# A decode block on one core: the down projection's first 20 row chunks in loads of 12 and 8

## The chip, the core and the metric

The kernel runs on one core of one Trainium2 chip. A core has five engines with a queue of instructions each: TensorE (PE; its weight loads are listed apart as PEld), VectorE (DVE), ScalarE (ACT), GpSimd (POOL) and SyncE (SP), which here issues nearly all DMAs. The DMAs run on 16 DMA engines; a DMA of 128 partitions gives each of them eight rows, and loads that are queued one behind the other are worked off in order. The time is device time of one execution in microseconds, the median of several runs. Before the change it is 265.09 us (three runs, 264.94 to 265.29).

## What is computed

One decode step of a transformer block for 8 sequences: layer norm, attention of one new token over the last 1024 cached keys and values (32 query heads, 4 key/value heads of 128), the output projection with a residual, a second layer norm, and a gated feed-forward part, all in float32. The change is in the last product, `h @ w_down`.

```python
def _B_ref(x, w_gate, w_up, w_down):
    g = jnp.einsum("bsd,df->bsf", x, w_gate)     # 8 x 1024 times 1024 x 3584
    u = jnp.einsum("bsd,df->bsf", x, w_up)
    h = _gelu(g) * u
    return jnp.einsum("bsf,fd->bsd", h, w_down)  # 8 x 3584 times 3584 x 1024

h  = x + _A_ref(_layernorm(x), k_cache, v_cache, wq, wo)
h2 = h + _B_ref(_layernorm(h), w_gate, w_up, w_down)
```

## The kernel before

Every weight is used once, so the kernel is a row of loads into one large buffer, `space`, of 32 slots of 1024 float32 per partition (a slot holds one chunk of 128 rows of `w_down`), with matmuls behind them. The order of loads on SP's queue is written out by hand: `wq`, `kt`, `v`, `wo`, the first set of gate and up weights (4 column blocks of 512), the second set (3 column blocks), then `w_down`. A load waits for the matmuls that last read the slots it overwrites; SP works in order, so a load behind a waiting one waits too.

**The second set of the feed-forward part.** The gate weights of the second set lie in slots 0 to 11, the up weights in slots 12 to 23 (`place` counts them, and `base` is 24). The matmuls of L377 read them. `used[0, 1]` marks the last up matmul of the first set, `used[1, 0]` the last gate matmul of the second, `used[1, 1]` the last up matmul of the second.

**The down projection.** `w_down` has 28 chunks. `PARTS` (L27) says how they are loaded: 8, 8, 4, 4, 2, 1, and the last chunk in two column parts (`ends`, L448). Before the change chunk q lies in slot (24 + q) mod 32: chunks 0 to 7 in slots 24 to 31 (they wait for `used[0, 1]`), 8 to 19 in slots 0 to 11 (`used[1, 0]`), 20 and up from slot 12 on (`used[1, 1]`, L428). The load that ends with chunk 19 (`SIDE`, L430) leaves out the last 320 columns of that chunk; they come in eight small loads on four partitions each into `w_side` (L436), which SP issues just ahead of that load. A line of `move` (L92) issues every other load.

**The matmuls.** `h` is transposed into `at` (L189, L398, L401). PE can work on four groups of 32 output columns of its array at once; a result then lies four times in `ya`, 32 partitions each. First, L453 adds the residual `h_sb` into groups 0 and 1. Then L463 takes two chunks at a time: four products (two chunks, two halves of 512 columns). In a "slow" pair (`SLOW`, L36) the two chunks use the same two groups one after the other, in other pairs all four groups work at once. Each float32 product is two matmul rows in the profile. Behind chunk 19 the products of `w_side` (L473) fill in the missing columns in groups 1 and 3. DVE copies `ya` to `d1` (L478), PE adds its four parts into `acc` (L483, with `add2`) and goes on with chunks 20 to 26 in four quarters of 256 columns; ACT copies `acc` to `most` (L494); the two parts of the last chunk go to `tb` and `ta` (L505), DVE adds them to `most` (L508), and two DMAs write the output.

Of the kernel before, what the change touches and what calls it, by code (L numbers as in the profile page):

```python
# [15 lines left out]
NQ = 4  # L16
CP = 32 // B
QW = D // NQ
N = 512
# [4 lines left out]
SETS = (NQ, DF // N - NQ)  # L24


PARTS = (8, 8, 4, 4, 2, 1)  # L27
SIDE = 19
SIDE_COLS = 320
SIDE_ROWS = (0, 16, 64, 80)  # L30
ENDS = (160, 96)
FOLD = 20
AHEAD = 3


SLOW = (*range(0, 8), 16, 17)  # L36


class Flow:
# [42 lines left out]
    def run(self, engine, make, *waits, mark=True):  # L82
        ins = self.start(engine, make, waits)
        if not mark:
            return None
        self.done[engine] += 1
        ins.then_inc(self.own[engine], 1)
        return self.own[engine], self.done[engine]
# [7 lines left out]
def decode_block(nc, x, wq, kt, v, wo, gu, dn, side, ends, outs):  # L96
# [9 lines left out]
    run, move = fl.run, fl.move  # L106
# [31 lines left out]
    ta, tb, ya = bank("ta", N), bank("tb", N), bank("ya", N)  # L138
# [21 lines left out]
    w_side = sb("w_side", 64, len(SIDE_ROWS), SIDE_COLS)  # L160
# [68 lines left out]
    for hf in range(2):  # L229
        w, w_in, wb = wq_t[hf]  # L230
        q_ps = (acc, tb)[hf]
        for c in range(NC):
            for j in range(NQ):
                tok = run("tensor", lambda e, c=c, j=j: e.matmul(  # L234
                    q_ps[32 * j:32 * j + 32, :], xt[c], w[:, c, j * N:(j + 1) * N],
                    start=(c == 0), stop=(c == NC - 1)),
                    w_in, x_ok, mark=(c == NC - 1 and j == NQ - 1))
        free[wb] = tok
        q_sb = sb(f"q{hf}", P, N)
        tok = run("vector", lambda e: e.tensor_scalar(q_sb, q_ps, scale, None, op0=ALU.mult), tok)  # L240
        acc_free = tok
        qt, tok = transposes(ta, q_sb, N // P, tok, ta_free)
# [10 lines left out]
    for hf in range(2):  # L253
        s_ps = big[hf]
        k_t, k_in, wb = load(kt[hf], f"kt{hf}", "s b k", s=2, b=B)
        for b in range(HB):
            for k0 in range(0, W, N):
                for r in range(NQ):
                    s, half = divmod(r, 2)
                    c0 = 32 * b + 160 * half  # L260
                    end = b == HB - 1 and k0 + N == W and r == NQ - 1
                    tok = run("tensor", lambda e: e.matmul(  # L262
                        s_ps[32 * r:32 * r + 32, k0:k0 + N], qz[hf][:, s, c0:c0 + 32],
                        k_t[:, s, half * HB + b, k0:k0 + N],
                        start=(b == 0), stop=(b == HB - 1)), k_in, q_ok[hf], mark=end)
# [31 lines left out]
    for hf in range(2):  # L297
# [8 lines left out]
        for c in range(KC):  # L306
            for r in range(NQ):
                s, half = divmod(r, 2)
                tok = run("tensor", lambda e: e.matmul(  # L309
                    o3[32 * r:32 * r + 32], pt[:, c, 32 * r:32 * r + 32],  # L310
                    v_t[:, s, c, half * HB:(half + 1) * HB, :],
                    start=(c == 0), stop=(c == KC - 1)),
                    v_in, ta_free, ya_free, mark=(c == KC - 1 and r == NQ - 1))
# [15 lines left out]
    for hf in range(2):  # L329
# [4 lines left out]
        for h in range(0, 2 * REP, 2):  # L334
            for r in range(NQ):
                e2, ch = divmod(r, 2)
# [24 lines left out]
    q0 = 0  # L361
# [51 lines left out]
    SLOTS = 2 * BUF // D  # L413
    base = place // D

    def slot(q):
        return (base + q) % SLOTS

    def rows_of(q):
        return ring[:, slot(q)]  # L420
# [3 lines left out]
    for i, n in enumerate(PARTS):  # L424


        a, b = slot(q0), slot(q0) + n
        clear = used[0, 1] if a >= base else used[1, 0] if b * D <= place // 2 else used[1, 1]  # L428
        assert b <= SLOTS and (a >= base or b <= base)
        if q0 <= SIDE < q0 + n:  # L430
            assert SIDE == q0 + n - 1

            side_in = fl.sem("w_side")
            for h, src in enumerate(side):
                p0 = h % 4 + 32 * (h // 4)
                fl.start("sync", lambda e: e.dma_start(w_side[p0:p0 + 13:4], src), [zero[-1]]).then_inc(  # L436
                    side_in, 16)
            side_in = side_in, 16 * len(side)
            here = move(f"wd{i}", space[:, a * D:b * D - SIDE_COLS], dn[i], clear)
        else:  # L440
            here = move(f"wd{i}", ring[:, a:b], dn[i], clear)
        arrived.update((q, here) for q in range(q0, q0 + n))
        q0 += n
# [14 lines left out]
    for q in range(0, FOLD, 2):  # L458
        for i in range(NQ):
            e2, ch = divmod(i, 2)  # L460
            r = ch if q in SLOW else i
            n = N - SIDE_COLS if (q + e2, ch) == (SIDE, 1) else N
            run("tensor", lambda e: e.matmul(  # L463
                ya[32 * r:32 * r + 32, 0:n], at[:, q + e2, :],
                rows_of(q + e2)[:, ch * N:ch * N + n],
                start=(r not in opened), stop=(q == FOLD - 2 and ch == 0)),
                arrived[q + e2], at_ok[(q + e2) * P >= SETS[0] * N],
                mark=False)
            opened.add(r)
            if n < N:  # L470
                for s in range(len(SIDE_ROWS)):
                    r = 1 + 2 * (s % 2)
                    tok = run("tensor", lambda e: e.matmul(  # L473
                        ya[32 * r:32 * r + 32, n:N], at_side[:, s, :], w_side[0:48, s, :],
                        start=False, stop=(s >= len(SIDE_ROWS) - 2)), side_in, side_ok,
                        mark=(s == len(SIDE_ROWS) - 1))
    d1 = sb("d1", P, N)
    d1_ok = run("vector", lambda e: e.tensor_copy(d1, ya), tok)  # L478

# [131 lines left out]
```

## Time and profile before

| | before |
|---|---|
| median of three runs | 265.09 us (264.94 to 265.29) |
| the profiled execution, its time | 265.01 us |
| its span, first to last instruction | 263.7 us |
| PE busy | 139.5 us (53%) |
| DVE, ACT, POOL busy | 24.0, 10.8, 5.5 us |
| HBM read | 111.18 MB, 422 GB/s over the span |
| mean granted PE clock | 0.812 of full speed |

The profile is one execution on the chip, in microseconds from its first instruction. A row of the timeline gives the start, the length, the engine and line, what ran, out<-in with shapes, how many, and in brackets the engine's idle time ahead of it with what ended that. "DMA w<-dn" is the landing of a load of `w_down`. SPq rows are the issue of a DMA by SP, not its transfer. The chain of waits goes back from the last instruction, at each step to what released it. A stretch of the table of stretches gives, after its length, the busy time of PE, PEld, DVE, ACT and POOL, then the granted PE clock (1.00 is full speed, 0.50 half), the DMA share and GB/s. DMA bytes are put down to the stretch in which a packet starts, so a short stretch can show a share over 1.

### The profile page before, as it was taken

Reading aid. Unit: us, or ns where it says so; the run is one execution under the profiler, and the core shown is the slowest. Engines: PE = TensorE matmul, PEld = TensorE weight load, DVE = VectorE, ACT = ScalarE, POOL = GpSimd, SP = SyncE. Lnnn points to the kernel's source line nnn. Section 1 sums busy time; section 2 is a strip of 40 time slices with the busy share of each in tenths; the row PEclk is TensorE's granted clock in tenths of the full one; section 3 lists DMA queues with packets and bytes.
Section 4 is the critical chain, followed back from the end, with each engine's and each line's share of the span. In section 5 each row is a group of like instructions: output and inputs, shape, how many; then the busy total and the mean of one; then the engine's idle time right before and its main releaser. Section 6 shows DMA issues by size and latency. Waiting matters only on the chain.

```text
span 263.7 us, 2091 instructions
## 1 busy us (share of the span) xinstructions
PE 139.5 (53%) x966; PEld 40.8 (15%) x966; DVE 24.0 (9%) x59; ACT 10.8 (4%) x16; POOL 5.5 (2%) x15
## 2 busy tenths in 40 slices
PE   0015806804905916806706807818509667489876
PEld 0011201201201301301202202112102111123122
DVE  0320100100010020200200100160000200010011
ACT  1110000000010020110000000020000000000000
POOL 8000000000000000000000000000000000000000
PEclk9999975985965895975975956986965959799999
DMA  8997999999799989989998999899899989999995
GB/s 318 482 457 338 477 477 390 408 467 477 328 467 477 450 358 457 470 378 437 457 477 348 450 467 457 378 437 477 380 410 447 477 358 472 413 423 442 403 413 203
DMA packets 3256, 111.44 MB, mean 423 GB/s; under 512 B 520, under 2 KB 776, under 8 KB 1072
## 3 DMA queue, kind: packets, MB, share of 16 engines
q1 hardware_dynamic: 3088, 111.23, 98.1%
q8 instruction: 7, 0.11, 0.2%
q10 hardware_dynamic: 160, 0.08, 0.1%
q14 instruction: 1, 0.01, 0.0%
HBM read 111.18 MB, written 0.13 MB: 422 GB/s over the span
## 4 chain that ended last, share of the span: by engine, by line
DMA 78%; PE 20%; SPq 1%; issue 0%; DVE 0%
DMA w<-gu 20%; DMA w<-wq 16%; DMA w<-kt 12%; DMA w<-wo 11%; DMA w<-v 11%; DMA w<-ends 9%; PE big L377 6%; PE big L262 4%; PE tb L234 4%; PE tb L309 3%; PE ya L337 3%; SPq L92 1%; PE tb L505 0%; PE ta L505 0%; DVE o_fin L508 0%
## 5 line engine op out<-in xcount | busy, mean ns | idle before, releaser
L377 PE MATMUL big<-w,ln_t 128*32 128x512 f32 x224 | 36.8, 742 | 21.0 <-DMA w<-gu 21.0
L262 PE MATMUL big<-w,qz 128*32 128x512 f32 x128 | 19.1, 762 | 20.0 <-DMA w<-kt 20.0
L337 PE MATMUL ya<-w,ot 128*32 128x512 f32 x128 | 18.2, 732 | 19.4 <-DMA w<-wo 19.4
L377 PEld LDWEIGHTS big<-w,ln_t 128*32 128x32 f32 x224 | 9.2, 133 | 47.1 <-issue 26.3
L463 PE MATMUL ya<-w,at 128*32 128x512 f32 (+1 forms) x80 | 13.4, 588 | 2.1 <-DMA w<-dn 2.1
L309 PE MATMUL tb<-w,pt 128*32 128x512 f32 x64 | 9.1, 733 | 9.9 <-DMA w<-v 9.9
L234 PE MATMUL tb<-w,ln_t 128*32 128x512 f32 x64 | 9.3, 749 | 9.1 <-DMA w<-wq 9.1
L309 PE MATMUL acc<-w,pt 128*32 128x512 f32 x64 | 8.7, 703 | 8.5 <-DMA w<-v 8.5
L234 PE MATMUL acc<-w,ln_t 128*32 128x512 f32 x64 | 8.7, 705 | 7.5 <-DMA w<-wq 7.5
L189 PE MATMUL ta<-ident,ln_xn 64*128 64x64 f32 x16 | 2.0, 294 | 19.3 <-DVE ln_xn L215 19.3
L262 PEld LDWEIGHTS big<-w,qz 128*32 128x32 f32 x128 | 4.9, 137 | 33.4 <-issue 23.4
L337 PEld LDWEIGHTS ya<-w,ot 128*32 128x32 f32 x128 | 5.1, 132 | 31.1 <-issue 31.1
L390 DVE TENSOR_TENSOR hm<-ge,big 128x512 f32<-128x512 f32 (+1 forms) x2 | 1.4, 685 | 56.8 <-PE big L377 56.8
L271 DVE TENSOR_REDUCE nmax<-big 128x1 f32<-128x1024 f32 x2 | 2.4, 1224 | 35.7 <-PE big L262 35.7
L273 ACT ACTIVATE p<-big,nmax 128x1024 f32<-128x1024 f32 x2 | 2.2, 1115 | 78.2 <-DVE nmax L271 78.2
L463 PEld LDWEIGHTS ya<-w,at 128*32 128x32 f32 x80 | 3.6, 109 | 11.8 <-issue 9.8
L309 PEld LDWEIGHTS tb<-w,pt 128*32 128x32 f32 x64 | 2.5, 130 | 15.9 <-issue 15.9
L189 PEld LDWEIGHTS ta<-ident,ln_xn 64*128 64x128 f32 x16 | 1.6, 192 | 20.1 <-DVE ln_xn L215 20.1
L234 PEld LDWEIGHTS tb<-w,ln_t 128*32 128x32 f32 x64 | 2.3, 135 | 15.5 <-DMA w<-wq 9.3
L309 PEld LDWEIGHTS acc<-w,pt 128*32 128x32 f32 x64 | 2.4, 126 | 14.1 <-issue 14.1
L234 PEld LDWEIGHTS acc<-w,ln_t 128*32 128x32 f32 x64 | 2.4, 126 | 13.1 <-issue 13.1
L483 PE MATMUL acc<-w,at 128*32 128x256 f32 x56 | 3.6, 382 | 0.3 <-DMA w<-dn 0.3
(78 smaller groups left out, 54.0 us busy)
## 6 DMA issues: line engine op xcount, KB each, us to landing
w<-gu SPq DMA_DIRECT2D x2, 6144.0 KB, 23.7
w<-dn SPq DMA_DIRECT2D x2, 4096.0 KB, 26.9
w<-dn SPq DMA_DIRECT2D x1, 2048.0 KB, 20.0
w<-dn SPq DMA_DIRECT2D x1, 1888.0 KB, 23.7
w<-dn SPq DMA_DIRECT2D x1, 1024.0 KB, 22.1
w<-dn SPq DMA_DIRECT2D x1, 512.0 KB, 22.9
w<-ends SPq DMA_DIRECT2D x1, 320.0 KB, 23.2
w<-ends SPq DMA_DIRECT2D x1, 192.0 KB, 23.2
```

Source lines behind the costliest of these rows:

```text
L92: self.start(engine, lambda e: e.dma_start(out, src), waits).then_inc(s, 16)
L189: tok = run("tensor", lambda e, i=i: e.transpose(t[:, i, :], src[:, i * P:(i + 1) * P], ident[:rows, :rows]), id_ok, ready, clear, mark=(i ...
L234: tok = run("tensor", lambda e, c=c, j=j: e.matmul(q_ps[32 * j:32 * j + 32, :], xt[c], w[:, c, j * N:(j + 1) * N], start=(c == 0), stop=(c ...
L262: tok = run("tensor", lambda e: e.matmul(s_ps[32 * r:32 * r + 32, k0:k0 + N], qz[hf][:, s, c0:c0 + 32], k_t[:, s, half * HB + b, k0:k0 + N ...
L271: tok = run("vector", lambda e: e.tensor_reduce(out=nmax, in_=s_ps, axis=AX.X, op=ALU.max, negate=True), tok)
L273: p_ok = run("scalar", lambda e: e.activation(p_sb, s_ps, AF.Exp, bias=nmax, accum_out=tot), tok)
L309: tok = run("tensor", lambda e: e.matmul(o3[32 * r:32 * r + 32], pt[:, c, 32 * r:32 * r + 32], v_t[:, s, c, half * HB:(half + 1) * HB, :], ...
L337: tok = run("tensor", lambda e: e.matmul(ya[32 * r:32 * r + 32, :], ot[:, 2 * hf * REP + h + e2].rearrange("p r b -> p (r b)"), w[:, h + e ...
L377: tok = run("tensor", lambda e: e.matmul(pair[32 * j:32 * j + 32, s, :], ht[c], w[:, c, j * N:(j + 1) * N], start=(c == 0), stop=(c == NC ...
L390: tok = run("vector", lambda e: e.tensor_mul(hm[:rows], ge[:rows], pair[:rows, 1, :]), tok, g_ok)
L463: run("tensor", lambda e: e.matmul(ya[32 * r:32 * r + 32, 0:n], at[:, q + e2, :], rows_of(q + e2)[:, ch * N:ch * N + n], start=(r not in o ...
L483: tok = run("tensor", lambda e: e.matmul(acc[32 * j:32 * j + 32, 0:QW], lhs(j), rhs(j), start=start, stop=stop), *waits, mark=(stop and j ...
```

## The change

The first 20 chunks come in two loads, of 12 and 8 chunks, and the slots are dealt anew: chunks 0 to 11 lie in slots 0 to 11 (they wait for the gate matmuls of the second set, `used[1, 0]`), chunks 12 to 19 in slots 24 to 31 (`used[0, 1]`). The load that leaves out the 320 columns is now the one of 8 chunks, and the small side loads are issued ahead of it. Three pairs (chunks 0 to 5) are slow instead of five (0 to 7, 16 and 17). The side products run after chunk 11 instead of after chunk 19, and both halves of the last pair end their accumulation.

```diff
-PARTS = (8, 8, 4, 4, 2, 1)
+PARTS = (12, 8, 4, 2, 1)
...
-SLOW = (*range(0, 8), 16, 17)
+SLOW = tuple(range(0, 6))
+SIDE_AT = 10
...
+    first = PARTS[0]
+    places = [*range(first), *range(base, SLOTS), *range(first, base)]
+
     def slot(q):
-        return (base + q) % SLOTS
+        return places[q]
...
         a, b = slot(q0), slot(q0) + n
         clear = used[0, 1] if a >= base else used[1, 0] if b * D <= place // 2 else used[1, 1]
...
-            run("tensor", lambda e: e.matmul(
+            tok = run("tensor", lambda e: e.matmul(
                 ya[32 * r:32 * r + 32, 0:n], at[:, q + e2, :],
                 rows_of(q + e2)[:, ch * N:ch * N + n],
-                start=(r not in opened), stop=(q == FOLD - 2 and ch == 0)),
+                start=(r not in opened), stop=(q == FOLD - 2)),
                 arrived[q + e2], at_ok[(q + e2) * P >= SETS[0] * N],
-                mark=False)
+                mark=(q == FOLD - 2 and i == NQ - 1))
             opened.add(r)
-            if n < N:
-                for s in range(len(SIDE_ROWS)):
-                    r = 1 + 2 * (s % 2)
-                    tok = run("tensor", lambda e: e.matmul(
-                        ya[32 * r:32 * r + 32, n:N], at_side[:, s, :], w_side[0:48, s, :],
-                        start=False, stop=(s >= len(SIDE_ROWS) - 2)), side_in, side_ok,
-                        mark=(s == len(SIDE_ROWS) - 1))
+        if q == SIDE_AT:
+            assert opened == set(range(NQ))
+            for s in range(len(SIDE_ROWS)):
+                r = 1 + 2 * (s % 2)
+                run("tensor", lambda e: e.matmul(
+                    ya[32 * r:32 * r + 32, N - SIDE_COLS:N], at_side[:, s, :], w_side[0:48, s, :],
+                    start=False, stop=False), side_in, side_ok, mark=False)
```

More of the change, by code (lines that the diff above doesn't have):

```diff
@@ L428, in decode_block @@
         clear = used[0, 1] if a >= base else used[1, 0] if b * D <= place // 2 else used[1, 1]
+        assert [slot(q) for q in range(q0, q0 + n)] == list(range(a, b))
         assert b <= SLOTS and (a >= base or b <= base)
```

## The prediction

> **What bounds the kernel now.** I read the page first, then the chain of waits in order of time, then the timeline of the last 60 us, then the table of stretches.
>
> ```profile
> span 263.7 us, 2091 instructions
> ...
> q1 hardware_dynamic: 3088, 111.23, 98.1%
> ...
> DMA 78%; PE 20%; SPq 1%; issue 0%; DVE 0%
> ...
> 204.72 22.76 DMA w<-gu
> ...
> 237.67 23.19 DMA w<-ends
> ```
>
> SP's queue keeps the 16 DMA engines busy for 98.1% of the span, and the chain that ends last ends in a transfer: the last weights are issued at 237.67 and land 23.19 us later, because everything queued before them has to pass first. The page's 20% for PE in the chain is how long PE holds a buffer before the next load may be issued; it is no gap in the stream as long as another load is queued. So the kernel is one stream of 111 MB, and the change is worth what it does to the stream, unless it lets the stream run dry or makes PE late behind it.
>
> How close PE is behind the stream, the timeline tells (start, length, what ran, and in brackets the idle time before it):
>
> ```profile
> 212.94 9.25 PE L377 MATMUL big<-w,ln_t 128*32 128x512 f32 x48 [3.30 <-DMA w<-gu]
> ...
> 227.53 8.76 PE L377 MATMUL big<-w,ln_t 128*32 128x512 f32 x48 [5.34 <-DMA w<-gu]
> ...
> 237.86 1.05 PE L453 MATMUL ya<-h_sb,spread 128*32 128x512 f32 x4
> ...
> 238.74 7.04 PE L463 MATMUL ya<-w,at 128*32 128x512 f32 x32
> ...
> 246.95 3.64 PE L463 MATMUL ya<-w,at 128*32 128x512 f32 x32 [1.17 <-DMA w<-dn]
> ...
> 251.57 2.77 PE L463 MATMUL ya<-w,at 128*32 128x512 f32 x16 [0.98 <-DMA w<-dn]
> ...
> 254.27 1.27 PE L473 MATMUL ya<-w_side,at_side 48*32 48x320 f32 x8
> ...
> 255.58 0.69 DVE L478 COPY d<-ya 128x512 f32<-128x512 f32 x1 [17.06 <-PE ya L473]
> ...
> 256.33 0.64 PE L483 MATMUL acc<-d,add 128*32 128x256 f32 x8 [0.79 <-DVE d L478]
> ...
> 256.78 1.91 PE L483 MATMUL acc<-w,at 128*32 128x256 f32 x32
> ...
> 258.86 1.07 PE L483 MATMUL acc<-w,at 128*32 128x256 f32 x16 [0.17 <-DMA w<-dn]
> ...
> 260.11 0.64 PE L483 MATMUL acc<-w,at 128*32 128x256 f32 x8 [0.17 <-DMA w<-dn]
> ...
> 260.82 0.37 ACT L494 COPY most<-acc 128x256 f32<-128x256 f32 x1 [22.00 <-PE acc L483]
> 260.90 0.48 PE L505 MATMUL tb<-w,at 128*32 128x160 f32 x8 [0.15 <-DMA w<-ends]
> 261.38 0.37 PE L505 MATMUL ta<-w,at 128*32 128x96 f32 x8
> 261.45 0.32 DVE L508 TENSOR_TENSOR o_fin<-most,tb 128x160 f32<-128x160 f32 x1 [0.74 <-PE tb L505]
> ...
> 261.82 0.25 DVE L508 TENSOR_TENSOR o_fin<-most,ta 128x96 f32<-128x96 f32 x1
> ```
>
> Before each of the last loads PE idles a little (0.17, 0.17, 0.15 us) and a DMA ends the wait. PE is behind the stream, with under half a microsecond to spare as the rows stand.
>
> **The change, part by part.** *One load fewer.* Sizes from the list of DMA issues (queue, count, size, us to landing):
>
> ```profile
> w<-gu SPq DMA_DIRECT2D x2, 6144.0 KB, 23.7
> w<-dn SPq DMA_DIRECT2D x2, 4096.0 KB, 26.9
> ...
> w<-dn SPq DMA_DIRECT2D x1, 1888.0 KB, 23.7
> ...
> out<-o_fin SPq DMA_DIRECT2D x1, 80.0 KB, 1.6
> ```
>
> The bytes stay. Before, the stream after the up load passes 4096, 4096 and 1888 KB; PE starts on what landed at 227.53, 246.95 (8192 KB in 19.42 us, 2.371 ns per KB) and 251.57 (1888 KB in 4.62 us, 2.447 ns per KB, with the eight small side loads in the same stretch). After, it passes 12 chunks, the size of a gate load, which took 14.59 us (212.94 to 227.53): landed at 242.12. Then 4096 - 160 = 3936 KB at 2.371: 9.33 us, landed at 251.45. That is 0.12 us ahead of 251.57. Bounds: the removed load cannot have cost more than the excess of its own stretch, 4.62 - 1888 x 2.371 = 0.14 us; and if the second load ran at the worse rate (9.63 us) everything would land 0.18 us later. I take 0.12 us earlier, since 3936 KB lies next to the 4096 KB row.
>
> *The first load is issued later.* SP's rows:
>
> ```profile
> 208.16 0.33 SPq L92 DMA_DIRECT2D w<-dn  x1
> ...
> 222.24 0.33 SPq L92 DMA_DIRECT2D w<-dn  x1
> ...
> 222.61 5.08 SPq L436 DMA_DIRECT2D w_side<-side  x8
> ...
> 227.73 9.42 SPq L92 DMA_DIRECT2D w<-dn  x3
> ```
>
> The 12 chunks go where the gate weights lay, so they wait for the gate's last matmul (222.19) and leave at 222.24; the issue at 208.16 falls away. Behind that wait on SP stand the side loads and the 8-chunk load, which takes the old third load's place at 227.73; none comes later than now. But from 204.72 to 222.24 the up load is the only thing queued. Does a DMA engine run dry? The row below is one of a table of 0.1 us stretches (busy PE, PEld, DVE, ACT and POOL, then granted clock, DMA share, GB/s); bytes count where a packet starts. Its 819 GB/s are 82 KB: one 48 KB row of the up load and the first 32 KB row of the down load, so the earliest engine turns to the down load at about 224.95.
>
> ```profile
> 224.90:225.00 0.10, 0.00 (x0) 0.00 (x0) 0.00 (x0) 0.00 (x0) 0.00 (x0) 1.00 1.90 819
> ```
>
> An 80 KB output needs 1.6 us from issue to landing with nothing queued, so the first bytes of the new load can be asked for by 222.24 + 1.6 = 223.84 at the latest, 1.1 us before an engine wants them. Cost 0; the cover is the up load's tail. Without it, the leading engines would idle first, and only a delay past the last engine's end (its data are in by 227.48) would move the end.
>
> *PE waits longer, then works less.* Now PE finds chunk 0 landed at about 237.2 (half of the 19.42 us after 227.53) and works on two column groups until 245.78. After the change it is done with the h_sb products at 238.91 and waits until 242.12 for chunk 0; queued behind are all chunks, the side products and d1. Timeline rows of PE include a drain: x8 starts 0.45 us after the row before it though its own length is 0.64, so 0.19 of each row overlaps the next. A pair on two groups takes (7.04 - 0.19)/4 = 1.71 us, on four (3.64 - 0.19)/4 = 0.86, the side products 1.08. Before: five slow pairs, five fast; after: three and seven, 1.70 us less. At full clock: 242.12 + 3 x 1.71 + 3 x 0.86 + 1.08 = 250.91, so the side products are over when chunk 12 lands at 251.45; then 3.64 us for four fast pairs: 255.09, where PE now ends at 255.54. PE gains 0.45 us there, and it is hidden: the chain behind d1 waits for loads anyway.
>
> *The clock after that wait.* This is the dangerous part. PE's granted clock in stretches of 3.41 us that end where the clock changes (first number: length; then PE busy; the number behind POOL: granted clock):
>
> ```profile
> 70.60:74.01 3.41, 1.38 (x16) 0.16 (x8) 1.22 (x1) 0.70 (x1) 0.00 (x0) 1.00 0.75 327
> 74.01:77.42 3.41, 0.00 (x0) 0.00 (x0) 0.39 (x2) 0.51 (x2) 0.00 (x0) 0.50 0.84 365
> 80.84:84.25 3.41, 2.10 (x12) 0.68 (x16) 0.00 (x0) 0.00 (x0) 0.00 (x0) 0.50 0.75 327
> 84.25:87.67 3.42, 3.42 (x20) 0.91 (x16) 0.00 (x0) 0.00 (x0) 0.00 (x0) 0.50 1.35 580
> 159.34:162.76 3.42, 2.98 (x16) 0.90 (x20) 0.00 (x0) 0.00 (x0) 0.00 (x0) 0.50 1.24 537
> 162.76:166.17 3.41, 3.41 (x36) 1.07 (x32) 0.00 (x0) 0.00 (x0) 0.00 (x0) 1.00 0.71 308
> 220.78:224.20 3.42, 1.40 (x12) 0.18 (x6) 0.00 (x0) 0.59 (x1) 0.00 (x0) 1.00 1.07 460
> 224.20:227.61 3.41, 0.08 (x3) 0.09 (x6) 0.00 (x0) 0.00 (x0) 0.00 (x0) 1.00 0.92 394
> ```
>
> At full clock, 1.38 us of work in a stretch lost the clock and 1.40 kept it. At half clock, 2.10 us did not win it back and 2.98 did. Counting on from 227.61 in steps of 3.413, the stretch 237.85 to 241.26 holds about 1.06 us of work after the change (now it is full): the clock halves at 241.26, before chunk 0 lands. The stretch 241.26 to 244.68 then holds 244.68 - 242.12 = 2.56 us, between 2.10 and 2.98 and a little nearer 2.98; I take it that full clock returns at 244.68. PE is late by half of 2.56: 1.28 us.
>
> How late may PE be? 0.54 us go in the wait for chunk 12 (250.91 to 251.45), 0.45 us are the gain at 255.09. Behind d1, PE's rows without drains from the start of the d1 products (256.33) to the end of chunk 26 are 0.45 + 1.72 + 0.88 + 0.45 + 0.19 = 3.69, then 0.07 and 0.37 for the copy to most; o_fin may start at 261.45 - 0.12 = 261.33, less 0.06 to start: the d1 products may start as late as 257.14, 0.81 later than now. Together 1.80 us, and 1.28 is less. Cost 0, bounds 0 and, with a second half-clock stretch (below), 1.19.
>
> The Trainium skill, in TensorE: Matmul & The Clock Gate, What's actually happening, has the clock drop after at least one idle window of about 3.4 us, by which a wait of 3.2 us would leave it alone; by that PE would be 1.28 us earlier, and the end the same. The stretch from 70.60 here shows a drop without a wholly idle window, so the measurement decides.
>
> **The sum.** The profiled execution took 265.01 us: 263.7 of span and 1.31 around it. It is 0.08 under the median of the runs, 265.09. Stream -0.12, late issue 0, PE 0: 264.89 for that execution, and 265.09 - 0.12 = 264.97, say 265.0, for the median.
>
> **Rivals.** *The clock stays down (slower).* If 2.56 us do not win it back, PE runs at half clock until 248.09 and is late by (248.09 - 242.12)/2 = 2.99 us; 1.80 are absorbed, the end moves by 1.19 - 0.12 = 1.07: 266.1. It decides from 1.80 us of lateness, that is 3.6 us of work at half clock. Where the stretches lie in another execution no row tells; shifting them by a full stretch gives costs only where the clock falls between about 240 and 241.6, at a lateness of 2.4 to 3.2 us: 265.5 to 266.3. For it: the bound 2.98. Against: in most positions the clock falls late enough that the next stretch is full of work, lateness 1.7 or less.
>
> *The stream runs dry.* If the 6 MB load needs far longer from issue to first byte than the output's 1.6 us: the last engine ends the up load by 227.48, so at 5.5 us from issue, say, the end comes about 0.3 us later, 265.3, and 1 us later for each further us. Against: the 1.1 us of margin even at the first engine.
>
> *A load costs a fixed time.* Then the removed load gives that back. In rows: the excess of a whole stretch is 0.14 us, so the removed load should give no more; were the true cost hidden by the rows and 2 us, the time would be 263.1. DMA: Bandwidth & Descriptors, in the Trainium skill, Anatomy of one DMA — SWDGE (gpsimd) path, fits about 2.0 us fixed per DMA on another issuing path; by it this is the gain. The queued loads here land at an even rate, so the rows speak against it.
>
> *PE sets the end.* If the small idles of 0.17 are artefacts and PE's chain is the bound, its 0.45 us count: 264.6. Against: a DMA ends each wait.
>
> *The change does nothing that shows*: the clock holds, the load was free: 265.1.
>
> **How the numbers follow.** About 0.2%, 0.53 us, is what a measurement of this kernel can tell from no change. Forecast 0.64 (265.0); clock stays down 0.19 (266.1, nearly all beyond 0.53); nothing shows 0.06; stream dry 0.03, counted slower for two thirds; fixed cost 0.03 (faster); PE sets the end 0.05 (on the border, half faster). Faster 0.03 + 0.025, with rounding 0.06; slower 0.19 + 0.02 = 0.21; same 0.73. The range, 264.6 to 266.1, takes in the border case and the clock case as priced at 266.1; the forecast's own is 264.7 to 265.3, from the bounds -0.14 and +0.18 and the runs' spread.
>
> **What would show it.** Right: the 8-chunk load issued at about 227.7; chunk 0's matmuls start at 242.1 with some 3.2 us of idle before them; the first of them at 0.50 clock, then 1.00; chunk 12's matmuls start between 251.4 and 251.9, with a DMA or PE ending the wait; the ends' loads still the last of the chain, near 260.8. DMA share before 227 without a hole. Wrong: clock 0.50 for two stretches, d1's copy after 256.4 and no idle before chunks 24 to 26; or a hole in the DMA share at 223 to 227.

## The result and the profile after

| | executions | median | lowest to highest |
|---|---|---|---|
| before | 22 | 265.18 us | 264.91 to 265.59 |
| after | 22 | 265.82 us | 264.96 to 266.5 |

The ratio of after to before is 1.0019 (95% interval 1.0011 to 1.0027): 0.5 us more (the medians lie 0.64 apart), where the forecast was 0.1 us less. The median hides the shape. Of the 22 executions after the change, 8 lie at 264.96 to 265.17, which is the forecast; 2 at 265.50 and 265.55; and 12 at 265.81 to 266.5. Nothing lies between 265.55 and 265.81. None of the 128 executions of the kernel before, these 22 and the 106 that ran beside the kernels below, came over 265.6. One execution of the series again5 below, 272.57 us at a granted clock of 0.64, was in a slower state and is counted nowhere.

The profiled execution after the change is one of the low ones, 264.96 us. From its page (span, SP's queue and the queue of instruction packets with packets, MB and share of the 16 DMA engines, the chain by engine):

```profile
span 263.6 us, 2089 instructions
...
q1 hardware_dynamic: 2944, 111.23, 98.1%
q8 instruction: 7, 0.11, 0.2%
...
DMA 78%; PE 20%; SPq 1%; issue 0%; DVE 0%
```

Its timeline (start, length, engine and line, what ran, in brackets the idle time ahead of it and what ended that; SPq rows are issues by SP):

```profile
221.66 0.33 SPq L93 DMA_DIRECT2D w<-dn  x1
...
227.52 9.87 PE L378 MATMUL big<-w,ln_t 128*32 128x512 f32 x48 [5.92 <-DMA w<-gu]
...
238.96 1.05 PE L458 MATMUL ya<-h_sb,spread 128*32 128x512 f32 x4
242.04 7.92 PE L468 MATMUL ya<-w,at 128*32 128x512 f32 x48 [2.03 <-DMA w<-dn]
249.89 1.27 PE L479 MATMUL ya<-w_side,at_side 48*32 48x320 f32 x8
251.39 3.63 PE L468 MATMUL ya<-w,at 128*32 128x512 f32 x32 [0.23 <-DMA w<-dn]
...
258.77 1.07 PE L488 MATMUL acc<-w,at 128*32 128x256 f32 x16 [0.55 <-DMA w<-dn]
260.03 0.64 PE L488 MATMUL acc<-w,at 128*32 128x256 f32 x8 [0.20 <-DMA w<-dn]
260.81 0.48 PE L510 MATMUL tb<-w,at 128*32 128x160 f32 x8
```

The chain of waits, start and length, shows what released that last row:

```profile
238.77 21.99 DMA w<-ends
260.76 0.04 issue
260.81 0.48 PE tb L510 x8
```

The stream is 0.1 us earlier: the `tb` products start at 260.81 instead of 260.90, as the last loads land. PE waits for chunk 0, for chunk 12 and for the last loads, each time for a DMA. In this execution the change does what was forecast, except that the clock did not fall in the wait for chunk 0. The table of stretches (length, busy PE, PEld, DVE, ACT and POOL, then granted clock, DMA share, GB/s) says why:

```profile
236.62:240.04 3.42, 2.52 (x18) 0.69 (x12) 1.24 (x2) 0.26 (x1) 0.00 (x0) 1.00 0.89 382
240.04:243.45 3.41, 1.41 (x8) 0.47 (x10) 0.00 (x0) 0.00 (x0) 0.00 (x0) 1.00 0.91 388
243.45:246.86 3.41, 3.41 (x24) 0.95 (x22) 0.00 (x0) 0.00 (x0) 0.00 (x0) 1.00 0.99 425
```

The up products (L378) had begun at half clock and ended at 237.4, so the wait was short, and its stretch still held 1.41 us of work, enough to keep the clock.

### The profile page after: what moved, and what is told of

It reads as the page before. It is cut to its first block, busy times and chain, and to the rows that moved or that the text cites. A ratio compares the mean times of both kernels' runs of the same rounds, so it can differ in the third digit from the quotient of the medians.

```text
span 263.6 us, 2089 instructions
## 1 busy us (share of the span) xinstructions
PE 137.2 (52%) x966; PEld 40.1 (15%) x966; DVE 24.0 (9%) x59; ACT 10.8 (4%) x16; POOL 5.5 (2%) x15
## 3 DMA queue, kind: packets, MB, share of 16 engines
q1 hardware_dynamic: 2944, 111.23, 98.1%
## 4 chain that ended last, share of the span: by engine, by line
DMA 78%; PE 20%; SPq 1%; issue 0%; DVE 0%
DMA w<-gu 20%; DMA w<-wq 16%; DMA w<-kt 12%; DMA w<-wo 11%; DMA w<-v 11%; DMA w<-ends 8%; PE big L378 6%; PE ya L338 4%; PE big L263 3%; PE tb L235 3%; PE tb L310 3%; SPq L93 1%; PE tb L510 0%; PE ta L510 0%; DVE o_fin L513 0%
## 5 line engine op out<-in xcount | busy, mean ns | idle before, releaser
L378 PE MATMUL big<-w,ln_t 128*32 128x512 f32 x224 | 36.0, 723 | 21.5 <-DMA w<-gu 21.5
L263 PE MATMUL big<-w,qz 128*32 128x512 f32 x128 | 17.8, 718 | 21.2 <-DMA w<-kt 21.2
L378 PEld LDWEIGHTS big<-w,ln_t 128*32 128x32 f32 x224 | 8.9, 130 | 47.2 <-issue 23.5
L310 PE MATMUL acc<-w,pt 128*32 128x512 f32 x64 | 9.7, 778 | 9.1 <-DMA w<-v 9.1
L235 PE MATMUL acc<-w,ln_t 128*32 128x512 f32 x64 | 9.8, 781 | 7.5 <-DMA w<-wq 7.5
L310 PE MATMUL tb<-w,pt 128*32 128x512 f32 x64 | 8.5, 690 | 8.8 <-DMA w<-v 8.8
L235 PE MATMUL tb<-w,ln_t 128*32 128x512 f32 x64 | 8.7, 705 | 8.0 <-DMA w<-wq 8.0
L468 PE MATMUL ya<-w,at 128*32 128x512 f32 (+1 forms) x80 | 11.6, 588 | 2.3 <-DMA w<-dn 2.3
```

The source lines that it names most:

```text
L235: tok = run("tensor", lambda e, c=c, j=j: e.matmul(q_ps[32 * j:32 * j + 32, :], xt[c], w[:, c, j * N:(j + 1) * N], start=(c == 0), stop=(c ...
L263: tok = run("tensor", lambda e: e.matmul(s_ps[32 * r:32 * r + 32, k0:k0 + N], qz[hf][:, s, c0:c0 + 32], k_t[:, s, half * HB + b, k0:k0 + N ...
L310: tok = run("tensor", lambda e: e.matmul(o3[32 * r:32 * r + 32], pt[:, c, 32 * r:32 * r + 32], v_t[:, s, c, half * HB:(half + 1) * HB, :], ...
L378: tok = run("tensor", lambda e: e.matmul(pair[32 * j:32 * j + 32, s, :], ht[c], w[:, c, j * N:(j + 1) * N], start=(c == 0), stop=(c == NC ...
L468: tok = run("tensor", lambda e: e.matmul(ya[32 * r:32 * r + 32, 0:n], at[:, q + e2, :], rows_of(q + e2)[:, ch * N:ch * N + n], start=(r no ...
```

## The experiments

Three theories stood at the start. **Clock (C):** in the upper executions the wait for chunk 0 costs PE two stretches at half clock, the rival of the prediction. **Stream (S):** the load of 12 chunks, issued late, sets the stream back. **Pairs (P):** the new order of pairs and side products itself takes longer. A fourth came up on the way (clock-by-groups): pairs on two column groups win the clock back less readily than pairs on four.

This table counts the executions of all kernels that ran more than once, the changed kernel's second series among them:

| | n | up to 265.2 | to 265.6 | over 265.6 | ratio to before (95%) |
|---|---|---|---|---|---|
| after | 22 | 8 | 2 | 12 | 1.0019 (1.0011 to 1.0027) |
| after, again5 | 11 | 4 | 2 | 5 | 1.0011 (1.0001 to 1.0021) |
| fill3 | 11 | 8 | 3 | 0 | 0.9998 (0.9989 to 1.0007) |
| fill3b | 11 | 5 | 5 | 1 | 1.0002 (0.9994 to 1.0011) |
| slow5 | 4 | 0 | 0 | 4 | 1.0079 (1.0061 to 1.0097) |
| split4 | 12 | 5 | 4 | 3 | 1.0019 (1.0005 to 1.0032) |
| fast0 | 12 | 4 | 6 | 2 | 1.0012 (0.9998 to 1.0026) |
| fastfirst | 11 | 6 | 3 | 2 | 1.0008 (0.9999 to 1.0016) |
| lateissue | 12 | 5 | 3 | 4 | 1.0016 (1.0000 to 1.0032) |
| fillgate | 11 | 5 | 2 | 4 | 1.0012 (1.0001 to 1.0023) |
| fillboth | 11 | 11 | 0 | 0 | 0.9994 (0.9985 to 1.0002) |

### The changed kernel again, four times

No edit; each of the four is one execution with its trace.

> The changed kernel once more, for a second profile. Its 22 executions lie in two heaps, 9 at 264.96 to 265.17 and 13 at 265.5 to 266.5. Theory C (clock): after PE's wait for chunk 0 the clock halves, and in the upper heap PE is late by more than the 1.8 us that can be absorbed. So an execution of the upper heap shows 0.50 over most of the 12 chunks' matmuls, no wait for chunk 12, d1's copy after 256.0, and the loads landed when they land in the first profile (chunk 0 at 242.0, last ends load near 260.8). Theory S (stream): the load issued 14 us later lets some DMA engines run dry; then chunk 0 or chunk 12 land later (after 242.5 or 252.0) while the clock is 1.00. Theory P (pairs): the new order of PE's work is itself too long; then PE is late at full clock too. An execution of the lower heap (4 in 10) tells nothing new.

> As the run before it: the changed kernel, a third profile. C: in the upper heap 0.50 clock over the 12 chunks, loads on time; S: loads late; P: PE late at 1.00. Where the half-clock stretches begin should differ between the profiles, since their phase differs by execution.

> The changed kernel once more, in search of an execution of the upper heap (13 of 22). C: if the time is above 265.4, the clock is 0.50 for two stretches from 240.4 to 242.0 on, chunks 0 to 11 take 10.2 to 11.2 us instead of 7.92, PE never waits behind chunk 12, and the loads land as in the other profiles. S: the loads land late.

> As the one before: if above 265.4, C says two stretches at 0.50 and loads on time, S says loads late at 1.00. If below, one stretch at most from 242.0 on, or none.

Measured: 264.96, 264.94, 265.43 and 265.81 us. The first two have one stretch at half clock, as forecast, though it begins 1.1 us after chunk 0 has landed (243.10 against 242.00) and not 0.9 us before. again1, table of stretches:

```profile
239.69:243.10 3.41, 1.22 (x8) 0.38 (x8) 0.00 (x0) 0.03 (x1) 0.00 (x0) 1.00 0.95 404
243.10:246.51 3.41, 3.41 (x10) 0.74 (x8) 0.00 (x0) 0.00 (x0) 0.00 (x0) 0.50 1.03 443
```

Its products of chunks 0 to 11 take 9.62 us instead of 7.92, PE is 1.70 us late, and from there to the end no row has idle time ahead of it that a DMA ends; the `tb` products start at 260.82, no later than in the first profile. So about 1.7 us are absorbed, and hardly more.

again4 caught the upper heap. Table of stretches, then timeline:

```profile
237.14:240.55 3.41, 1.37 (x10) 0.32 (x8) 0.56 (x1) 0.26 (x1) 0.00 (x0) 1.00 0.92 394
240.55:243.96 3.41, 2.05 (x6) 0.55 (x8) 0.00 (x0) 0.00 (x0) 0.00 (x0) 0.50 1.10 470
243.96:247.38 3.42, 3.42 (x10) 0.73 (x8) 0.00 (x0) 0.00 (x0) 0.00 (x0) 0.50 1.03 442
```

```profile
221.65 0.33 SPq L93 DMA_DIRECT2D w<-dn  x1
...
227.38 8.50 PE L378 MATMUL big<-w,ln_t 128*32 128x512 f32 x48 [5.78 <-DMA w<-gu]
...
237.46 1.05 PE L458 MATMUL ya<-h_sb,spread 128*32 128x512 f32 x4
241.91 10.61 PE L468 MATMUL ya<-w,at 128*32 128x512 f32 x48 [3.40 <-DMA w<-dn]
252.45 1.27 PE L479 MATMUL ya<-w_side,at_side 48*32 48x320 f32 x8
253.65 3.63 PE L468 MATMUL ya<-w,at 128*32 128x512 f32 x32
...
257.36 0.69 DVE L483 COPY d<-ya 128x512 f32<-128x512 f32 x1 [19.23 <-PE ya L468]
...
258.10 0.64 PE L488 MATMUL acc<-d,add 128*32 128x256 f32 x8 [0.82 <-DVE d L483]
258.56 3.21 PE L488 MATMUL acc<-w,at 128*32 128x256 f32 x56
261.58 0.46 PE L510 MATMUL tb<-w,at 128*32 128x160 f32 x8
```

Chunk 0 landed on time (241.91), so S is out for this execution, and the instructions are those of again1, so P is too. The clock fell at 240.55, before chunk 0; the 2.05 us of work left in that stretch did not win it back, and a second one passed at half clock. The products take 10.61 us, PE is 2.69 us late, and the waits for chunk 12 and for chunks 24 to 26 are gone: 2.69 less the prediction's 1.80 is 0.89 on top of 264.9, which is the 265.8 measured. The clock had come back early, at 230.31, inside the up products, so these ended early and left the longest wait, 3.40 us. It is what the prediction named as its sign of being wrong: two stretches at 0.50, d1's copy after 256.4 (here at 257.36) and no idle time before chunks 24 to 26.

again3's time (265.43) is none of this: its gate products (L378) begin at 213.35 instead of 212.99 and all loads stay 0.4 to 0.5 us late, so that was lost upstream of the change.

### Filling the wait

```diff
+    for _ in range(3):
+        run("tensor", lambda e: e.matmul(
+            big[1][0:32, 0:512], spread.rearrange("p r b -> p (r b)"), h_sb[:, 0:512],
+            start=True, stop=True), h_ok, consts, mark=False)
     opened = {0, 1}
```

Three products into a bank that nothing reads, ahead of chunk 0.

> The changed kernel with three extra products of 512 columns into an unused bank between the h_sb products and chunk 0, some 2.6 us of PE work in the wait; their result is not read. C: the clock stays at 1.00, the upper heap is gone, all executions 264.9 to 265.3, median 265.07, ratio 0.9996 against the kernel before (the load saved, 0.1 us). S: as without them, 6 in 10 above 265.4, median 265.8, ratio 1.002. P: as S or worse.

> The changed kernel with three products of 512 columns into an unused bank ahead of chunk 0, once more. Clock theory: no stretch is lost in the wait, nothing above 265.6, median 264.9 to 265.1, 0 to 0.25 us under the kernel before. Stream theory: two heaps as in the changed kernel on the same chip.

Measured: 264.98 and 265.23 us; one of 22 executions over 265.6, where the changed kernel has 17 of 33. From fill3's table of stretches, the one that now holds the wait:

```profile
240.19:243.60 3.41, 3.41 (x13) 1.11 (x13) 0.00 (x0) 0.00 (x0) 0.00 (x0) 1.00 0.97 413
```

Work was added and time went away. The wait's clock makes most of the upper heap. Nine of the 22 still lie above 265.2, one of them at 265.85, which was not expected.

### More and less work behind the wait

```diff
-SLOW = tuple(range(0, 6))
+SLOW = tuple(range(0, 10))      # slow5
+SLOW = ()                       # fast0
+SLOW = tuple(range(6, 12))      # fastfirst
```

> The changed kernel with five slow pairs instead of three (chunks 0 to 9): 1.7 us more PE work ahead of chunk 12, loads untouched. C: at full clock PE is done at 252.5 instead of 250.8, 1.1 us after chunk 12 lands, still absorbed behind d1, so the lower heap stays at 265.1; but every half-clock stretch now costs what it makes PE late: upper heap 266.5 to 268.2, and most executions in it, median above 266.5. S: heaps and median as in the changed kernel, 265.8. P: all executions later by up to 1.7 us, in one heap.

> The changed kernel with no slow pairs: 2.57 us less PE work on chunks 0 to 11, loads untouched, the wait for chunk 0 as long as before. C: lateness of up to 3.2 us from the wait for chunk 0 is now covered (1.80 + 2.57 = 4.4), so no execution at 265.8 to 266.5 from it; but PE then waits up to 3.1 us for chunk 12, and a clock that halves there makes d1 late by up to 1.7 where 1.26 is covered: some executions 0.3 to 0.5 later, median 265.0 to 265.4. S: the upper heap stays, 6 in 10 at 265.5 to 266.5, median 265.8.

> Same work, same wait ahead of chunk 0, but the three pairs behind that wait use four column groups and the three after them two. Clock theory (only the work time that a stretch holds counts): the upper heap stays, about half of the executions above 265.4, median within 0.3 us of that of the changed kernel on the same chip. Rival, clock-by-groups: the pairs on four groups win the clock back, so at most two in ten lie above 265.4, median 265.0. Stream theory: no difference.

slow5: 267.2 us, all four executions from 266.62 up; the lower heap at 265.1 that was expected beside them did not show. Two pairs more on two groups take 1.7 us of the slack, and the one stretch at half clock is then paid nearly in full: the `tb` products start 1.53 us later than in again1. Its timeline has no wait left:

```profile
241.95 11.33 PE L468 MATMUL ya<-w,at 128*32 128x512 f32 x48 [2.09 <-DMA w<-dn]
...
259.32 3.21 PE L488 MATMUL acc<-w,at 128*32 128x256 f32 x56
262.35 0.46 PE L510 MATMUL tb<-w,at 128*32 128x160 f32 x8
```

fast0: 265.28 us, fewer over 265.6 (2 of 12), as more slack should give; those two lie at 266.54 and 266.9, which was not expected and has no trace. fastfirst: 265.2 us, 4 of 11 over 265.4. In its traced execution the half-clock stretch costs what it costs with the slow pairs in front (9.62 us for chunks 0 to 11), which speaks against clock-by-groups; the shares, 2 of 11 over 265.6 against 5 of 11 on the same chip, are too close to settle it.

### Moving the wait

split4 puts the first 20 chunks in loads of 4, 8 and 8:

```diff
-PARTS = (12, 8, 4, 2, 1)
+PARTS = (4, 8, 8, 4, 2, 1)
-    first = PARTS[0]
+    first = PARTS[0] + PARTS[1]
```

> The changed kernel with its first load cut in two, 4 and 8 chunks, in the same slots and order, so three loads again and chunk 0 landed near 232.4. PE finds work at 238.9. C: no long wait (two slow pairs 238.9 to 242.3, then chunks 4 to 11 at 242.1), no upper heap, median 265.15 as before the change, ratio 1.000. S: the load is still issued at 222, so the upper heap stays, median 265.8. P: the order of pairs and side products is that of the changed kernel, so the upper heap stays.

265.35 us, and three executions at 266.19 to 266.75: the expected end of the heap did not come. Table of stretches and timeline:

```profile
247.87:251.28 3.41, 0.00 (x0) 0.00 (x0) 0.00 (x0) 0.00 (x0) 0.00 (x0) 1.00 0.94 394
251.28:254.69 3.41, 3.24 (x16) 0.79 (x20) 0.00 (x0) 0.00 (x0) 0.00 (x0) 0.50 1.02 435
```

```profile
238.65 7.95 PE L468 MATMUL ya<-w,at 128*32 128x512 f32 x48
246.53 1.27 PE L479 MATMUL ya<-w_side,at_side 48*32 48x320 f32 x8
251.45 5.22 PE L468 MATMUL ya<-w,at 128*32 128x512 f32 x32 [3.66 <-DMA w<-dn]
```

PE no longer waits for chunk 0; it waits 3.66 us ahead of chunk 12 instead and loses the clock there, nearer the end, with less behind it to absorb the loss. This execution took 265.18 us; that the three above 266 lost two stretches there is likely but not shown, they have no trace.

late_a, late_b and late_c hold the whole stream back at the program's start, to shift the wait against the stretches: the first weights are issued behind one of the memory clears at the start.

```diff
-    wq_t = [load(wq[0], "wq0", "c n", c=NC)]
...
-    wq_t.append(load(wq[1], "wq1", "c n", c=NC))
...
     zero = [run("gpsimd", lambda e, t=t: e.memset(t, 0.0)) for t in (*qz, h_sb, w_side)]
+    free[0] = x_zero      # late_a; zero[0] in late_b, zero[1] in late_c
+    wq_t = [load(wq[hf], f"wq{hf}", "c n", c=NC) for hf in range(2)]
```

> The changed kernel with its first load held back until x_sb is zeroed: the whole stream about 1.0 us later, everything else the same. In the three profiles of the changed kernel so far a stretch ends 239.6 to 240.0 us from the start, and the clock's stretches do not move with the program. If they stand there again, counted from the first load they now end 1.0 us earlier, that is at 238.6 to 239.0 and at 242.0 to 242.5, where chunk 0 lands. C: the clock halves there, one stretch of full work follows, PE is late by 1.7 us, which is absorbed: time 264.95 + 1.0, the span's end 1.0 later. S and P: 1.0 later too, or an upper-heap time by chance.

> As the one before with the first load held back about 2.0 us. Counted from the first load a stretch ends near 241.0 (240.9 to 241.5). C: the clock halves there, 1 us or less before chunk 0's matmuls; the next stretch holds 2.3 to 2.8 us of work. If that does not win the clock back, PE is late by 2.8 us and the end comes about 1.1 us later than 264.95 + 2.0; if it does, the end is 264.95 + 2.0. S and P: no tie between the hold and the excess.

> Held back about 2.6 us. Counted from the first load a stretch ends near 240.4 to 240.9. C: the clock halves there and the next stretch holds only 1.8 to 2.3 us of work, which does not win it back: two stretches at 0.50, PE late by 2.6 us, the end 0.8 to 1.0 us later than 264.95 + 2.6, with no wait for chunk 12 and none before chunks 24 to 26. S and P: no tie between the hold and the excess; at 1.00 clock S shows late loads, P late PE.

265.92, 266.79 and 267.73 us. The position did not come out as meant: the stretches of 3.41 us keep step within an execution, but they are not tied to the program's start, so their place cannot be set this way. With the hold taken off (0.95, 1.89 and 2.47 us, by the start of chunk 0's products against the first profile: 242.99, 243.93 and 244.51) the three are at 264.97, 264.90 and 265.26, with one, none and one stretch at half clock behind the wait, nearly all of it absorbed (late_c's 0.3 us come from its loads, as the next section shows). late_c gives a bound for winning the clock back, 2.77 us of work at half clock:

```profile
243.87:247.28 3.41, 2.77 (x8) 0.74 (x10) 0.00 (x0) 0.00 (x0) 0.00 (x0) 0.50 0.98 420
```

bench runs 20 blocks of products with a DVE-made wait in each behind the down projection, three pairs of every second block on two groups.

> The changed kernel with 20 extra blocks of PE work on data in place ahead of the last chunk, results not read: seven pairs on four groups, the two h_sb products, a wait of about 3 us made by four DVE copies, then six pairs; in even blocks the first three are slow (two groups), in odd blocks none. Some 330 us longer. It shows what the clock does at 20 positions of its stretches. C as predicted: after such a wait the clock halves in nearly all blocks, a stretch with 2.3 to 2.8 us of work at half clock wins it back, the same for two groups as for four, and about one block in four has two half-clock stretches. C': work on two groups counts less, so a stretch of slow pairs that is not full does not win it back and in about half or more of the even blocks two stretches stay at 0.50, in the odd ones far fewer. S and P say nothing of it: the clock stays at 1.00 in most blocks.

604.06 us, inconclusive: two blocks, one of each kind, last 34.0 us, about ten stretches, so the blocks fall into step with them and show only a few positions. The clock fell behind 9 of the 20 waits, for one stretch each, where nearly all were expected. Of fast against slow pairs it says nothing.

### The second cause: the late issue

> The changed kernel as it is, in many executions beside the kernel before on one chip. Clock theory, and the rival that pairs on two column groups win the clock back less readily (clock-by-groups): two heaps again, about half of the executions at 264.9 to 265.2 and about half at 265.4 to 266.5, median between 265.1 and 265.9. Stream theory: one heap.

again5 confirms the two heaps (ratio 1.0011, 5 of 11 over 265.6). Its traced execution, 266.52 us, is not explained by the clock. Timeline, then the chain of waits:

```profile
212.86 9.95 PE L378 MATMUL big<-w,ln_t 128*32 128x512 f32 x48 [4.29 <-DMA w<-gu]
...
222.87 0.33 SPq L93 DMA_DIRECT2D w<-dn  x1
...
242.10 9.62 PE L468 MATMUL ya<-w,at 128*32 128x512 f32 x48 [2.50 <-DMA w<-dn]
...
260.40 1.86 PE L488 MATMUL acc<-w,at 128*32 128x256 f32 x24 [0.57 <-DMA w<-dn]
262.43 0.48 PE L510 MATMUL tb<-w,at 128*32 128x160 f32 x8 [0.16 <-DMA w<-ends]
```

```profile
238.36 24.02 DMA w<-ends
262.38 0.04 issue
262.43 0.48 PE tb L510 x8
```

PE had one stretch at half clock (9.62), as in again1, and waits for DMAs again at the end: the last loads took 24.02 us instead of 21.99. In the records of the single DMA packets, the last rows of 15 DMA engines end by 260.9, those of one engine at 262.4. The same records show one odd row of the load of 12 chunks: the DMA engines turn to that load from 225.0 on, a row of 48 KB takes 1.82 us, and here one takes 3.88. By the time of the load's issue, with the time from there to the first row of the earliest engine:

```
execution     issued    first row    rows of the load of 12 that took over 1.9 us
again1..4     221.4 to 222.0   3.3 to 3.7 later   none
after, fill3, fill3b   221.7   3.3 to 3.4 later   none
late_a, late_b   222.35, 223.57   3.7, 3.3 later   none
lateissue     222.42   2.8 later   225.23 us: 2.02,  225.48 us: 2.45
fastfirst     222.68   2.4 later   225.05 us: 2.10,  225.66 us: 2.04
fast0         222.79   2.3 later   225.07 us: 3.19,  225.31 us: 1.98
again5        222.87   2.2 later   225.10 us: 3.88
late_c        224.79   2.6 later   227.39 us: 1.95,  227.51 us: 2.63,  227.64 us: 2.30
```

What a slow row costs depends on its engine. In the first profile six engines finish the load of 8 chunks 1.3 to 1.9 us ahead of the other ten, so they have that much to spare. Followed row by row, the engine of the slow row in again5 has used this up: it finishes that load at 251.01, level with the last of the others (250.97). Then a second thing falls on the same engine, one of the seven 16 KB packets of the queue that the page lists as `q8 instruction`:

```
                                    first profile    again5
its engine ends the load of 8       249.05 us        251.01 us
the last of the 16 engines          250.86 us        251.01 us
the instruction packet              250.88, 1.03 us  252.84, 0.92 us
the 16 KB row of w_down behind it   251.90, 1.16 us  253.75, 1.16 us   (others 0.61)
```

It costs the engine about 1.5 us both times; in the first profile the lead covers that, in again5 nothing does, and the last rows land 1.6 us late. The slow row alone would have moved the end by hardly anything. In fastfirst (265.31 us) and late_c a slow row alone puts one engine 0.4 us behind all others at the end of the load of 8, and the last rows come about 0.4 us late.

The gate products set the issue: they run at half clock for two stretches in again5 (9.95 us, against 8.61 in the first profile). That a load issued late isn't ready when the first engines turn to it is a reading of the table; it doesn't say why only one to three of the 16 first rows are slow, while others that begin as early (225.04 in again5) take 1.82 us. Three kernels test it:

```diff
-            here = move(f"wd{i}", ring[:, a:b], dn[i], clear)
+            here = move(f"wd{i}", ring[:, a:b], dn[i], clear, g_ok if i == 0 else None)   # lateissue, beside fill3's products
...
+            if (k, s) == (1, 0):                                                          # fillgate; fillboth: beside fill3's
+                for _ in range(3):
+                    run("tensor", lambda e: e.matmul(
+                        big[1][0:32, 0:512], spread.rearrange("p r b -> p (r b)"), h_sb[:, 0:512],
+                        start=True, stop=True), h_ok, consts, clear, mark=False)
```

> The changed kernel with the three filling products ahead of chunk 0 and one wait more: the load of 12 chunks is issued behind ScalarE's gelu of the second set, some 0.65 us later, at 222.1 to 223.5. Late-issue theory (issued after about 222.65, the load isn't ready when the first DMA engine turns to it at 225.05; that engine's first row took 2.10, 3.19 and 3.88 us instead of 1.82 in three executions, at issues of 222.68, 222.79 and 222.87): at least half of the executions above 265.4, some at 266 to 267, median 265.3 or more; if the profiled one is issued after 222.65, its first row takes over 2 us. Clock theory alone: as with the filling products before, median 265.0 to 265.25, at most two in eleven above 265.6.

> The changed kernel with three filling products ahead of the second set's gate products and none ahead of chunk 0. The gate stage then runs at full clock and the load of 12 chunks is issued between 220.6 and 221.8. Late-issue theory: no slow first row; what is left above 265.6 is the clock's two stretches behind the wait for chunk 0, a fifth to a third of the executions, none above 266.4; median 265.0 to 265.2. Clock theory alone: half of the executions above 265.4, as in the changed kernel.

> Both fillings. If the two causes together make the upper heap: nothing above 265.5, median 264.85 to 265.0, 0.1 to 0.25 us under the kernel before. If a third cause is at work, one in five or more above 265.5.

lateissue: 265.31 us, 4 of 12 over 265.6, the highest 267.31; fill3 with the same filling has 1 of 22. That is the expected median, though fewer than half lie over 265.4 (4 of 12, one at 265.40). Its traced execution has two slow rows, though it is issued ahead of the expected limit of 222.65, and still ends at 264.93: a slow row costs nothing in some executions.

fillgate: 265.21 us. The gate products take 7.07 us at full clock, the load leaves at 220.09 (0.5 us earlier than expected), no row is slow, and the executions fall into two clean heaps: 7 at 264.89 to 265.22, 4 at 265.9 to 266.31. The traced one (265.9) is of the upper heap and repeats again4. Table of stretches, then timeline:

```profile
237.14:240.55 3.41, 1.44 (x11) 0.37 (x9) 0.56 (x1) 0.26 (x1) 0.00 (x0) 1.00 0.92 397
240.55:243.96 3.41, 1.90 (x6) 0.56 (x8) 0.00 (x0) 0.00 (x0) 0.00 (x0) 0.50 1.09 467
243.96:247.38 3.42, 3.42 (x12) 0.74 (x8) 0.00 (x0) 0.00 (x0) 0.00 (x0) 0.50 1.03 442
```

```profile
242.06 10.54 PE L473 MATMUL ya<-w,at 128*32 128x512 f32 x48 [3.48 <-DMA w<-dn]
```

fillboth: 265.05 us, all 11 executions at 264.85 to 265.16, the narrowest of all kernels here. With both waits filled no upper heap is left, so filling both is enough: none of the 11 lies above 265.2, against 9 of 22 with the wait for chunk 0 filled alone. The median is just above the expected 264.85 to 265.0. It is the version to take from the changed ones; against the kernel before (0.9994, 0.9985 to 1.0002) a gain of 0.1 us can't be told from none.

## Why the prediction was wrong, step by step

**The bound and the stream: right.** The stream ends 0.1 us earlier (0.12 forecast), chunk 0 landed at 242.04 (242.12) and chunk 12 at 251.39 (251.45). A third of the executions show the forecast's time. None of the traced ones gets there on the forecast's path, a clock that falls before chunk 0 lands and comes back after one stretch: they lose no stretch or a full one after the landing, and the 1.70 us of the full one fit into the slack of 1.80 with little to spare, which is in part luck.

**The pairs and side products: right.** At full clock they leave 0.23 us of wait for chunk 12 (0.54 forecast, of which 0.19 is the drain that the sum leaves out); the gain of PE is hidden.

**The slack of 1.80 us: right.** 1.70 us late cost nothing in again1, again2 and late_a; 2.69 us cost 0.85.

**The clock after that wait: the step that failed.** It counted on from the stretches of one execution, took full clock to return at 244.68, and gave two half-clock stretches 0.19, "in most positions the clock falls late enough". But the position differs in every execution. The prediction's own range for a costly fall, 240 to 241.6, is nearly half of a stretch of 3.41 us, so with no row to say where the stretches lie the chance should have been near 0.4. I also held the end of the up products fixed while moving the stretches. That end moves with the same clock: the `h_sb` products start at 237.46 in again4 and at 238.96 in the first profile. In the two traced executions of the clock's upper heap, again4 and fillgate's, the clock comes back early in the up products (230.31), the wait is longest, and the clock falls before chunk 0 lands. One position gave the likely case; three are common: no half-clock stretch, one (both near 265.0) and two. The rival's mechanism and price (265.5 to 266.3) were right, 265.81 and 265.9 in the two traced executions; its chance was too small. The stretch that decides was judged at 2.56 us, between 2.10 and 2.98: measured, 2.05 and 1.90 us did not win the clock back and 2.77 did, so that reading may stand. What failed is the position, and with it the share of the executions that lose two stretches: 4 of 11 in fillgate, whose traced load left early (220.09).

**The late issue at cost 0: wrong in part.** The cover of 1.1 us came from an output's 1.6 us and one issue time, 222.24. The gate's clock moves the issue between 221.4 and 222.9. Where the earliest engine turned to the load 3.3 us or more after the issue, no row was slow; where it turned 2.8 us or less after it, some first rows were. So up to an issue of 222.0 the step holds. Later, an engine can lose the lead it has, which agrees with the prediction's remark that only a delay past the last engine's end would move the end; what moved it by 1.6 us in again5 was the instruction packet on that engine as well, a term that the sum did not have. The rival "the stream runs dry" named the place, but for all engines at once and at 0.03.

**The others** fell: the removed load gave 0.1 us and no fixed cost, PE doesn't set the end in the low heap, and the change does show.

Of the heap above 265.6, 17 of 33 in the changed kernel, fillgate leaves 4 of 11 and fill3 1 of 22. So the clock behind the wait is the larger part and the late issue the smaller. That the late issue takes part is shown by the traces of again5 and fastfirst; lateissue (4 of 12 over 265.6) and fillboth (none of 11 over 265.2) against fill3 (1 and 9 of 22) agree. fillgate's 4 of 11 alone can't be told from 17 of 33. Their exact shares, why fast0 has two executions above 266.5 and lateissue one, and why only some of the first rows are slow stay open.

## What to carry to other kernels

A tight loop of loads can hide a wait of 3 us ahead of the matmuls in one execution and not in the next, because the wait's price is a clock that is decided on a grid that nothing here could place: work the change out for every position of the grid, with everything before it that runs on the same clock moved too, and give each outcome its share. Where a wait of that length can't be avoided, products that nobody reads took the loss away here at no measured cost. And a load that is issued into a queue with only one other load in it has no fixed cover: give the issue the spread that its trigger has. A DMA engine's lead over the others is slack too, and what else runs on that engine spends it.

## What the runs showed of the hardware

The stretches of 3.41 us lie differently in each execution and are not tied to the program's start. At full clock a stretch kept the clock with 1.41 us of busy PE and lost it with 1.22, 1.37 and 1.44 (the last two with transposes in them), so the profile's busy time gives no sharp limit; at half clock 1.90 and 2.05 us did not win it back, 2.77 did. The Trainium skill, in TensorE: Matmul & The Clock Gate, What's actually happening, has the clock drop after an idle window: here it drops after windows with 1.22 to 1.44 us of work in them.

A DMA engine that turned to a 6 MB load 2.2 us after its issue (222.87 to 225.10) spent 3.88 us on a row of 1.82; another, at 225.04, took the usual 1.82. The Trainium skill, in DMA: Bandwidth & Descriptors, Specifications, gives about 0.6 us to the first byte on SyncE's path; under a full stream a row was still slow where its engine turned to the load 3.1 us after the issue (lateissue, 225.48).

An instruction packet of 16 KB takes about 1.5 us from the one DMA engine on which it runs: 1.03 us itself in the first profile and 0.92 in again5, and the row of 0.61 behind it takes 1.16 in both.

One engine of 16 that is late by 1.6 us moves the end by as much: every load waits for its slowest engine, and a DMA share of 97.5% instead of 98.1% over the span is all that the page shows of it.
